# Spare matrix products of a one-core kernel moved: eleven groups more ahead of the first scores, thirteen fewer later

## The chip, the core and the metric

The kernel runs on one core of a Trainium2 chip. A core has five engines that run side by side: TensorE (matrix products, the page's PE, with its weight loads as PEld), VectorE (DVE), ScalarE (ACT), GpSimd (POOL) and SyncE (SP), which here only issues transfers. Each engine takes its instructions in the order in which they were written for it, and waits at an instruction until the data it needs are there. The metric is the device time of one execution in microseconds, as the median of several runs. Beside it there is a profile of one execution.

## The reference

Two blocks in a row. The first is a gated linear recurrence over 768 tokens for 4 sequences and 8 heads of width 48:

```
f = 1 / (1 + exp(-f_logit))
for t in range(S):
    state = f[t] * state + outer(k[t], v[t])
    y[t]  = q[t] @ state
```

The second takes the heads' outputs side by side as x (4 x 768 x 384), mixes with a two-dimensional Fourier transform, and ends in a two-layer network with a residual:

```
mixed = real(fft(fft(x, tokens), channels))
u  = x + mixed
un = (u - mean(u)) / sqrt(var(u) + 1e-6)
out = u + relu(un @ w_ch1) @ w_ch2
```

All values are f32; w_ch1 is 384 x 1536 and w_ch2 1536 x 384.

## The kernel before, in words

The recurrence is done in 16 units, each two heads of one sequence, and 6 chunks of 128 tokens. Of one unit, `attention` computes: the gate's logarithm (ScalarE, L330 and L331), its running sum W (a VectorE scan, L337), the exponentials (ScalarE, L342, L343, L345), q and k scaled with them (VectorE, L349 and L350), and the scores within a chunk (48 small products on TensorE, L361, into two PSUM buffers), which VectorE copies under a causal mask (L368). Then `outputs`: TensorE turns k (L506), ScalarE copies it out (kT, L508), TensorE forms the chunks' states (ds, L517), VectorE runs them through a scan (stt, L525), TensorE adds up y from the scores (L537) and from the states (L544), ScalarE copies y out (L553 to L557), TensorE turns it (yt, L564), ScalarE copies that into x (L566), and `fold` prepares sums and differences for the Fourier transform (L590 to L612, VectorE and GpSimd).

Once the four units of a sequence are through, `fnet` does the transform as products with tables (z, L650; mix, L669), adds it to x (L725, L728), and normalises (L691 to L709); `projected` does the network: the first layer L750 with its ReLU on ScalarE (L752), the second L759 or, in blocks, L773. The weights are loaded in a raw form by SyncE (L267) and converted (ScalarE L238, VectorE L240 and L241, GpSimd L242).

The buffers tie these together. g and k have three buffers for the units to come, q four, W and kT two each, and the scores, states and turned matrices share two PSUM buffers. A load of a later unit is issued by SyncE only once the earlier unit has done with the buffer, and all loads behind it in SyncE's order wait too.

The order of all work is written out by hand in the string ORDER. Each word runs one step and so adds its instructions to the engines' queues: a number is the next step of that unit, F, H and P are steps of `fnet`, of the normalisation and of `projected` for a sequence, L are loads, r, R fetch raw weights, C converts one block of them, T and S bring the tables, W combines weights. The word D calls `busy`, which issues four products whose results are never used:

```
for _ in range(4):
    nc.tensor.matmul(spare, lhsT=bound[:, :C], rhs=bound[:, :2 * C], start=not started, stop=True,
                     skip_group_check=True)
```

They are 128 x 128 by 128 x 256 in bf16. Their output is 256 columns of the PSUM area that also holds y; the operand, `bound`, is ready once GpSimd has filled it (L138). A group that stands behind a unit's y products waits, in the kernel as built, for ScalarE's last copy of that y (L557). Nothing reads what they write; their purpose is to keep TensorE busy while it would otherwise stand still.

Of the kernel before, what the change touches and what calls it, by code (L numbers as in the profile page):

```python
# [12 lines left out]
C = 128  # L13
# [11 lines left out]


ORDER = (
    "Gq2 r I D Gq0 L0f Gk1 L1f D Gk0 L0q i D Gq3 C Gq1 Z L0k 0 D 1 Gk2 0 L1q 1 L1k D 0 0 1 0 r 1 L2f 0 2 "
    "C L1v 1 L3fk D 1 3 L0v 0 1 L2q 2 0 0 r D 1 L2k 3 1 0 2 r 3 L3q 2 L2v D 0 C L3v D C L4fk R D 4 2 2 3 "
    "1 0 C 2 4 1 3 L5qv D L4qv L5fk 3 D D 3 2 0 2 3 2 3 C r 4 1 4 L6fk C r 2 5 4 D L6qv 4 D 2 1 5 6 3 4 "  # L30
    "D 4 C 5 3 D T 3 6 4 5 5 4 2 r L7fk 7 5 D L7qv 3 5 S L8fk C 4 7 6 6 5 F0 5 r r F0 F0 F0 7 4 C F0 "
    "L9fk 5 6 8 H0 H0 6 5 6 r D D H0 D C L8qv 6 7 L9qv P0 6 7 r C P0 7 7 C 9 P0 r r 5 8 C r C F0 r 7 F0 "
    "6 P0 5 9 C 6 7 P0 r C P0 8 8 C P0 r r 7 P0 P0 8 9 H0 C P0 P0 8 7 8 C P0 H0 7 D 9 6 H0 H0 C 9 r C P0 "
    "9 L10fk r 9 P0 r C 9 L11fk 10 C 6 P0 11 4 P0 P0 P0 P0 P0 P0 10 P0 P0 P0 L10qv P0 P0 7 F1 9 P0 F1 H0 "
    "9 W P0 D P0 P0 11 F1 P0 L11qv P0 P0 P0 9 P0 P0 P0 8 L12fk P0 11 11 8 P0 P0 10 11 F1 P0 11 11 10 "
    "L14fk F1 8 P0 14 F1 P0 10 P0 8 10 P0 P0 H1 H1 10 L12qv P0 P0 10 P0 F1 P0 11 11 10 P0 10 H1 P0 P0 P0 "
    "P0 12 12 12 P0 P0 12 P0 H1 P0 12 P0 H1 L13fk P1 P1 P1 P1 P1 14 13 P1 12 8 8 P1 P1 12 9 10 L13qv 13 "
    "P1 P1 L14qv 9 P1 12 11 P1 H1 11 10 P1 P1 13 P1 13 P1 12 P1 P1 14 P1 14 V 13 P1 c V 10 P1 P1 P1 P1 "
    "P1 V L15fk P1 13 P1 11 V P1 P1 P1 P1 c P1 11 F2 V c F2 F2 H1 13 H1 F2 c 14 P1 c V c P1 P1 12 P1 P1 "
    "14 P1 P1 13 V V V P1 15 F2 c P1 12 P1 P1 P1 P1 c P1 H2 14 15 V V P1 P1 P1 P1 P1 13 P1 14 F2 P1 c P1 "  # L40
    "P1 15 V 13 P1 H2 P1 P1 L15qv P1 14 13 P1 V 12 H2 F2 14 P2 P2 P2 P2 P2 P2 P2 15 P2 P2 P2 c c 12 H2 V "
    "H2 15 H2 15 P2 c P2 15 P2 P2 15 P2 14 13 15 P2 P2 14 P2 P2 15 13 P2 P2 P2 P2 P2 H2 V 15 P2 P2 14 15 "
    "H2 P2 P2 P2 P2 15 F3 F3 P2 F3 F3 P2 F3 c P2 P2 P2 P2 P2 V P2 c P2 V c c V P2 P2 P2 P2 P2 c P2 F3 F3 "
    "P2 V P2 H3 P2 P2 P2 H3 H3 P2 P2 P2 P2 P2 P2 P2 P2 P2 P2 P3 H3 c P3 P3 P3 P3 V P3 c P3 P3 P3 c V V c "
    "P3 P3 P3 H3 P3 P3 P3 P3 P3 P3 c P3 P3 V P3 H3 P3 P3 P3 P3 P3 P3 H3 H3 P3 P3 P3 P3 P3 P3 P3 P3 P3 P3 "
    "P3 P3 V P3 P3 P3 P3 P3 c P3 c P3 P3 P3 M P3 P3 P3 P3 P3 P3 P3 P3 P3 P3 P3 P3"
)

PAIRS = ((0, 3), (2, 5), (1, 4))
# [925 lines left out]
```

## Time and profile before

| | |
|---|---|
| median time | 557.96 us (3 runs, 557.95 to 559.05) |
| span of the profiled execution | 556.9 us |
| mean granted TensorE clock | 0.976 of full |
| TensorE busy | 529.4 us (95%), 4194 products |
| VectorE busy | 299.8 us (54%) |
| ScalarE busy | 192.6 us (35%) |
| GpSimd busy | 95.4 us (17%) |
| spare products (L153) | 92, from 3.9 to 155.6 us, 16.4 us busy in all |

The profile's page has the span in 40 slices of 13.9 us, with each engine's busy share of a slice in tenths, the clock that TensorE was granted, and the busy share of the 16 transfer engines. A timeline gives instructions with start and duration in us and, in brackets, the idle time of the engine ahead of them with the instruction or transfer that released it. A busy matrix engine isn't always at full speed: the same product takes longer at a lower clock, so durations and the clock are read together.

Where the 23 words D of the kernel before stand in the trace: five from 3.9 to 8.4 us; one each at 19.2, 22.8 and 25.4 us; two at 28.9; three at 38.1; two at 49.0; one each at 54.1, 58.6 and 62.8; two at 86.0 and one at 87.2; one each at 119.8 and 155.0 us.

### The profile page before, as it was taken

To read this page: it belongs to the slowest core of one execution; us is meant where nothing else is said; L and a number is where in the kernel's file an instruction comes from. 1 tells how busy PE (TensorE), PEld (TensorE's weight loads), DVE (VectorE), ACT (ScalarE), POOL (GpSimd) and SP (SyncE) were. 2 spreads that over 40 slices of the span, in tenths; PEclk is the share of its full clock that TensorE was granted. 3 is DMA by queue.
4 is the path that set the end of the run, shared out by engine and by line. 5 is a ranking of instruction groups with operands and counts; after the bars stand their busy time and mean duration, and the time that the engine had idled before them with its cause. 6 is when DMAs were issued, how large, how long until landed. Compare 5 with 4: busy or idle time off the path is not lost.

```text
span 556.9 us, 10217 instructions
## 1 busy us (share of the span) xinstructions
PE 529.4 (95%) x4194; PEld 464.4 (83%) x4194; DVE 299.8 (54%) x534; ACT 192.6 (35%) x497; POOL 95.4 (17%) x147
## 2 busy tenths in 40 slices
PE   3988699999999999999999999999999999999995
PEld 2877578886889889889889899899889798989985
DVE  8989899994845626445554443453443342413231
ACT  6757476573313433443240331321421302121110
POOL 6136642634101000140200000103001000010000
PEclk9788889999999999999999999999999999999999
DMA  8969636343402010310630301102002005000000
GB/s 223 257 172 245 195 106 172 126 145 106 118 1 58 15 44 2 115 44 23 219 114 15 114 1 51 36 1 87 1 28 86 0 2 171 0 29 0 29 2 34
DMA packets 18398, 44.38 MB, mean 80 GB/s; under 512 B 3109, under 2 KB 4710, under 8 KB 18342
## 3 DMA queue, kind: packets, MB, share of 16 engines
q1 hardware_dynamic: 17094, 39.89, 25.4%
q0 software_dynamic: 1104, 3.54, 1.8%
q8 instruction: 35, 0.57, 0.4%
q14 instruction: 21, 0.17, 0.1%
q10 hardware_dynamic: 144, 0.20, 0.1%
HBM read 38.90 MB, written 4.72 MB: 78 GB/s over the span
## 4 chain that ended last, share of the span: by engine, by line
PE 85%; DMA 7%; DVE 4%; ACT 1%; SPq 1%; issue 1%; POOL 0%; ACTq 0%; DVEq 0%; POOLq 0%
PE up L750 34%; PE fx L773 15%; PE fz L773 12%; PE z L650 4%; DMA g<-in_qkf_dram 3%; PE po L759 3%; PE mix L669 3%; PE sc L361 3%; PE y L537 3%; PE y L544 3%; DMA k<-in_qkf_dram 2%; PE ds L517 2%; PE pt L708 1%; PE yt L564 1%; DMA tab<-in_seq_tab_dram 1%; PE st L506 1%
## 5 line engine op out<-in xcount | busy, mean ns | idle before, releaser
L750 PE MATMUL up<-unT,w 128*128 128x256 f32 x864 | 197.1, 382 | 1.5 <-DVE x L728 0.9
L750 PEld LDWEIGHTS up<-unT,w 128*128 128x128 f32 x864 | 161.3, 190 | 25.7 <-issue 1.5
L752 ACT ACTIVATE h<-up 128x256 f32<-128x256 f32 x144 | 55.1, 383 | 200.5 <-PE up L750 194.3
L617 POOL DMA_INDIRECT out_dram<-x,place x16 | 16.9, 1056 | 270.7 <-DVE x L803 235.2
L773 PE MATMUL fx<-block,h 128*128 128x192 f32 x264 | 46.5, 326 | 0.0
L773 PE MATMUL fx<-w,h 128*128 128x192 f32 x264 | 44.9, 327 | 0.1
L773 PEld LDWEIGHTS fx<-w,h 128*128 128x128 f32 x264 | 43.1, 190 | 0.8 <-ACT h L752 0.4
L773 PEld LDWEIGHTS fx<-block,h 128*128 128x128 f32 x264 | 43.5, 190 | 0.0
L242 POOL TENSOR_TENSOR w<-w,raw 128x384 uint32<-128x384 uint32 x24 | 29.0, 1211 | 51.8 <-ACT raw L238 21.3
L780 DVE TENSOR_TENSOR s<-h,h 128x768 f32<-128x768 f32 x11 | 10.5, 954 | 50.8 <-ACT h L752 50.8
L361 PE MATMUL sc<-q,W 48*64 48x128 f32 x768 | 28.1, 297 | 6.7 <-DVE W L350 5.2
L368 DVE COPY_PREDICATED at<-causal,sc 128x768 f32<-128x768 uint32 x32 | 31.4, 1033 | 4.2 <-PE sc L361 4.1
L361 PEld LDWEIGHTS sc<-q,W 48*64 48x64 f32 x768 | 23.9, 147 | 10.8 <-DVE W L350 5.6
L337 DVE TENSOR_TENSOR_SCAN W<-g,bound 112x768 f32<-112x768 f32 x16 | 28.3, 1767 | 1.2 <-PE st L506 0.9
L725 DVE TENSOR_TENSOR x<-mix,x 128x384 f32<-128x384 f32 x12 | 6.7, 556 | 39.1 <-PE mix L669 39.1
L537 PE MATMUL y<-at,v 128*64 128x128 f32 (+1 forms) x384 | 24.9, 278 | 0.0
L537 PEld LDWEIGHTS y<-at,v 128*64 128x64 f32 (+1 forms) x384 | 21.3, 132 | 3.0 <-issue 3.0
L153 PE MATMUL y<-bound 128*128 128x256 bf16 x92 | 16.4, 334 | 7.6 <-POOL bound L138 3.9
L773 PE MATMUL fz<-w,s 128*128 128x192 f32 x132 | 23.5, 328 | 0.0
L773 PE MATMUL fz<-block,h 128*128 128x192 f32 x132 | 23.5, 328 | 0.0
L773 PE MATMUL fz<-w,h 128*128 128x192 f32 x132 | 23.4, 327 | 0.0
L544 PE MATMUL y<-q,stt 48*48 48x128 f32 x320 | 22.1, 283 | 0.0
(145 smaller groups left out, 742.9 us busy)
## 6 DMA issues: line engine op xcount, KB each, us to landing
raw<-in_w_ch_dram SPq DMA_DIRECT2D x24, 384.0 KB, 4.4
g<-in_qkf_dram SPq DMA_DIRECT2D x32, 144.0 KB, 4.1
q<-in_qkf_dram SPq DMA_DIRECT2D x32, 144.0 KB, 4.0
k<-in_qkf_dram SPq DMA_DIRECT2D x32, 144.0 KB, 4.3
v<-in_v_dram SPq DMA_DIRECT2D x16, 288.0 KB, 4.7
k<-in_w_ch_dram SPq DMA_DIRECT2D x12, 384.0 KB
g<-in_w_ch_dram SPq DMA_DIRECT2D x12, 384.0 KB, 5.1
out_dram<-x SPq DMA_DIRECT2D x4, 168.0 KB
```

What stands on the lines that cost most here:

```text
L242: nc.gpsimd.tensor_tensor(bits, bits, lo, ALU.add)
L337: nc.vector.tensor_tensor_scan(W, g, bound[:R], 0.0, ALU.add, ALU.min)
L361: nc.tensor.matmul(ps[64 * s:64 * s + 64, r, i * C:(i + 1) * C], lhsT=W[ROWS[r], o + 64 * s:o + 64 * s + 64], rhs=Q[ROWS[r], o:o + C], sta ...
L368: nc.vector.copy_predicated(AT[:, :, half], causal.bitcast(U32).unsqueeze(1).unsqueeze(1).to_broadcast([128, 2, NCH // 2, C]), ps[:, :, :N ...
L537: nc.tensor.matmul(y[FILL[r], c * C:(c + 1) * C], lhsT=vt[:, c, r * D:r * D + (64 if r == 0 else D)], rhs=AT[:, r, c], start=(c % 4 == 0), ...
L544: nc.tensor.matmul(y[ROWS[r], c * C:(c + 1) * C], lhsT=st[ROWS[r], :, c - 1], rhs=Q[ROWS[r], c * C:(c + 1) * C], start=False, stop=True, s ...
L617: nc.gpsimd.indirect_dma_start(out=out.rearrange("b s d -> (b s) d"), out_offset=bass.IndirectOffsetOnAxis(ap=place[:, b, i:i + 1], axis=0 ...
L650: nc.tensor.matmul(z[:, cols], lhsT=src[:, j, lo:hi], rhs=tab[:, t, T % 2, cols], start=(i == 0), stop=(i == len(parts) - 1), skip_group_c ...
L669: nc.tensor.matmul(mix[:, o], lhsT=zz[:rows_of[T], T, PLACES[c]], rhs=cd[:rows_of[T], T, :NQ - odd], start=(i == 0), stop=(i == 1))
L750: nc.tensor.matmul(pp[:, :256], lhsT=w1[:, kt, m * 128:(m + 1) * 128], rhs=unT[:, kt], start=(kt == 0), stop=(kt == 2))
L752: nc.scalar.activation(hs[-1][:, m % H].rearrange("p t n -> p (t n)"), pp[:, :256], AF.Relu)
L773: nc.tensor.matmul(out, lhsT=h[:, m], rhs=blocks[i][:, m], start=(start and m == 0), stop=(m == H - 1), skip_group_check=True)
```

## The change

Only the words D of ORDER move; all others keep their order. The fifth D, the one ahead of the first scores (`L1k D 0 0 1`), becomes twelve in a row, so that 64 spare products in place of 20 stand between the start and the first scores. Of the eighteen words after that, thirteen are taken out (those at 19.2, 22.8, 25.4, 28.9, 49.0, 58.6, 86.0, 87.2, 119.8 and 155.0 us), and five stay (three at 38.1, and those at 54.1 and 62.8 us). In all there are 21 words in place of 23, and 84 products in place of 92.

The intention is to keep TensorE working without a gap from the first moments up to the first scores, so that its clock is up when they come, and to spare the products where they stand in real work's way.

```diff
 ORDER = (
-    "Gq2 r I D Gq0 L0f Gk1 L1f D Gk0 L0q i D Gq3 C Gq1 Z L0k 0 D 1 Gk2 0 L1q 1 L1k D 0 0 1 0 r 1 L2f 0 2 "
-    "C L1v 1 L3fk D 1 3 L0v 0 1 L2q 2 0 0 r D 1 L2k 3 1 0 2 r 3 L3q 2 L2v D 0 C L3v D C L4fk R D 4 2 2 3 "
-    "1 0 C 2 4 1 3 L5qv D L4qv L5fk 3 D D 3 2 0 2 3 2 3 C r 4 1 4 L6fk C r 2 5 4 D L6qv 4 D 2 1 5 6 3 4 "
-    "D 4 C 5 3 D T 3 6 4 5 5 4 2 r L7fk 7 5 D L7qv 3 5 S L8fk C 4 7 6 6 5 F0 5 r r F0 F0 F0 7 4 C F0 "
-    "L9fk 5 6 8 H0 H0 6 5 6 r D D H0 D C L8qv 6 7 L9qv P0 6 7 r C P0 7 7 C 9 P0 r r 5 8 C r C F0 r 7 F0 "
-    "6 P0 5 9 C 6 7 P0 r C P0 8 8 C P0 r r 7 P0 P0 8 9 H0 C P0 P0 8 7 8 C P0 H0 7 D 9 6 H0 H0 C 9 r C P0 "
-    "9 L10fk r 9 P0 r C 9 L11fk 10 C 6 P0 11 4 P0 P0 P0 P0 P0 P0 10 P0 P0 P0 L10qv P0 P0 7 F1 9 P0 F1 H0 "
-    "9 W P0 D P0 P0 11 F1 P0 L11qv P0 P0 P0 9 P0 P0 P0 8 L12fk P0 11 11 8 P0 P0 10 11 F1 P0 11 11 10 "
...
+    "Gq2 r I D Gq0 L0f Gk1 L1f D Gk0 L0q i D Gq3 C Gq1 Z L0k 0 D 1 Gk2 0 L1q 1 L1k D D D D D D D D D D D "
+    "D 0 0 1 0 r 1 L2f 0 2 C L1v 1 L3fk 1 3 L0v 0 1 L2q 2 0 0 r 1 L2k 3 1 0 2 r 3 L3q 2 L2v 0 C L3v C "
+    "L4fk R 4 2 2 3 1 0 C 2 4 1 3 L5qv D L4qv L5fk 3 D D 3 2 0 2 3 2 3 C r 4 1 4 L6fk C r 2 5 4 L6qv 4 2 "
+    "1 5 6 3 4 D 4 C 5 3 T 3 6 4 5 5 4 2 r L7fk 7 5 D L7qv 3 5 S L8fk C 4 7 6 6 5 F0 5 r r F0 F0 F0 7 4 "
+    "C F0 L9fk 5 6 8 H0 H0 6 5 6 r H0 C L8qv 6 7 L9qv P0 6 7 r C P0 7 7 C 9 P0 r r 5 8 C r C F0 r 7 F0 6 "
+    "P0 5 9 C 6 7 P0 r C P0 8 8 C P0 r r 7 P0 P0 8 9 H0 C P0 P0 8 7 8 C P0 H0 7 9 6 H0 H0 C 9 r C P0 9 "
+    "L10fk r 9 P0 r C 9 L11fk 10 C 6 P0 11 4 P0 P0 P0 P0 P0 P0 10 P0 P0 P0 L10qv P0 P0 7 F1 9 P0 F1 H0 9 "
+    "W P0 P0 P0 11 F1 P0 L11qv P0 P0 P0 9 P0 P0 P0 8 L12fk P0 11 11 8 P0 P0 10 11 F1 P0 11 11 10 L14fk "
...
```

The rows left out hold no word D; they are the same words, moved along by the breaks of the lines.

## The prediction

> **What bounds the kernel now.** I read the page's 40 slices first. A slice is 13.9 us.
>
> ```profile
> PE   3988699999999999999999999999999999999995
> DVE  8989899994845626445554443453443342413231
> PEclk9788889999999999999999999999999999999999
> DMA  8969636343402010310630301102002005000000
> ...
> L153 PE MATMUL y<-bound 128*128 128x256 bf16 x92 | 16.4, 334 | 7.6 <-POOL bound L138 3.9
> ```
>
> From the sixth slice on TensorE is full. VectorE is nearly full through the first nine, to about 125 us. The first five slices (to 70 us) are bound by nothing steadily: TensorE has holes, its clock falls, and the transfers fill their engines. So a microsecond of TensorE work removed after 125 us is worth a microsecond; between 75 and 125 us only what VectorE can follow; before 70 us it depends on which wait ends last. The 92 spare products (23 words D of 4) lie in all three parts. TensorE's timeline for the opening:
>
> ```profile
> 3.94 4.43 PE L153 MATMUL y<-bound 128*128 128x256 bf16 x20 [3.94 <-POOL bound L138]
> 13.53 5.71 PE L361 MATMUL sc<-q,W 48*64 48x128 f32 x96 [5.16 <-DVE W L350]
> 19.18 1.04 PE L153 MATMUL y<-bound 128*128 128x256 bf16 x4
> 20.00 2.04 PE L506 MATMUL st<-ident,W 112*128 112x112 f32 x10
> ...
> 28.89 1.86 PE L153 MATMUL y<-bound 128*128 128x256 bf16 x8 [1.63 <-ACT yT L557]
> 30.68 2.21 PE L361 MATMUL sc<-q,W 48*64 48x128 f32 x48
> ```
>
> The columns are start, duration, instruction, and idle time before it with its releaser. Twenty spare products, a hole of 5.2 us, then the scores of units 0 and 1. At 28.89 eight spare products wait for ScalarE's copy of the outputs (L557) and hold the scores of unit 2 behind them. Next, the granted clock by stretch (columns: busy time of PE, PEld, DVE, ACT, POOL, then PEclk, DMA share and GB/s):
>
> ```profile
> 11.80:13.50 1.70, 0.00 (x0) 0.00 (x0) 1.68 (x2) 1.68 (x3) 0.00 (x0) 0.50 1.11 277
> 13.50:19.30 5.80, 5.73 (x97) 5.00 (x98) 5.65 (x7) 5.19 (x9) 0.83 (x1) 0.50 1.04 245
> ...
> 28.70:32.10 3.40, 3.21 (x36) 2.40 (x39) 1.09 (x3) 2.34 (x7) 2.21 (x2) 0.50 0.70 164
> ...
> 66.20:73.10 6.90, 5.17 (x42) 3.70 (x39) 6.52 (x16) 5.74 (x13) 4.62 (x12) 0.51 0.54 159
> ```
>
> Half clock from 11.8 to 21.9, 28.7 to 32.1, 49.2 to 52.6 and 66.2 to 73.1 us: about 24 us. Then, in the timeline of all engines, who stands where around 31 us:
>
> ```profile
> 27.15 0.95 DVE L350 TENSOR_TENSOR W<-W,k 112x768 f32<-112x768 f32 x1
> ...
> 30.94 0.84 ACT L330 ACTIVATE g<-g 112x768 f32<-112x768 f32 x1 [1.03 <-DMA g<-in_qkf_dram]
> ...
> 32.31 1.96 DVE L368 COPY_PREDICATED at<-causal,sc 128x768 f32<-128x768 uint32 x2 [2.49 <-PE sc L361]
> ```
>
> The factors that unit 2's scores need are there at 28.10 (L350); VectorE then idles 2.49 us for scores that start only at 30.68. Last, the chain that ended last, which goes through a transfer just ahead of the dense part:
>
> ```profile
> 56.30 10.72 DMA g<-in_qkf_dram
> 67.10 0.94 ACT g L330 x2
> ```
>
> [...] the stretches above last 10.1, 3.4, 3.4 and 6.9 us, multiples of 3.4. [...] The trace: (4.43 - 0.27)/19 = 219 ns each in the first twenty, (0.61 - 0.27)/3 = 113 ns at 22.75 us. So the first twenty ran cold although the clock column shows 1.00 there; I believe the durations. [...] here ScalarE's copy of kT at 68.82 indeed stands behind the L330 that waits for the transfer above.
>
> **The change part by part.** The words other than D keep their order exactly, so each engine's other instructions do too; D goes from 23 to 21 words, 92 to 84 products. Five words to the first scores become 16 in one run; of 18 later, five stay.
>
> *Eleven groups more before the first scores.* 44 products. The first twenty end at 8.37 as now. [...] Then 44 x 113 ns = 5.0 us, ending at 13.4, beside L350, which ends at 13.48 and lets the scores go: nothing on the path. [...] 32 would be cold and 32 warm: 3.94 + 32 x 0.219 + 32 x 0.113 = 14.6 us, 1.1 us late. Even then scores at warm pace (48 in 1.54 us at 47.51) give the first half by 15.4, when VectorE, busy without a break, reaches L368 (15.32). Cost 0 to 0.1 us; I take 0.
>
> *The removed group at 19.18.* Warm, unit 1's scores end as soon as L368 frees their buffers (about 18.2, now 19.24), and the transposes L506 of unit 0 start when L368 frees the next, about 19.3 instead of 20.00. VectorE waits 0.9 us for them before the scan L337 at 21.24. That goes: 0.9 us.
>
> *Those at 22.75 and 25.38* (0.45 us each) lie inside VectorE's chain: 0.
>
> *The two at 28.89.* With them gone the scores wait only for L350: 28.10 - 0.9 = 27.2 instead of 30.68, 3.5 us earlier. Not all of it goes on: the g of unit 4 lands at 30.94 out of transfers that have filled their engines since 4 us, and ScalarE's queue holds it (L330, L331 to 32.75) ahead of the copies L566 (35.11 now), L508 and L553 to L557. They can move by 35.11 - 32.75 = 2.4 us at most, while the chain through scores and L368 moves 3.4. The y products of unit 1 (end 36.83), which release SyncE's load of q at 36.86, move between these too, and with it the transfers that now pause from 34 to 38 us. I take 2.9, the middle.
>
> *Those at 48.98 and 58.63.* VectorE is busy 4.75 of 5 us and 4.97 of 5 in 50 to 60: 0, apart from the clock. The kept ones (38.06, 54.14, 62.81) cost as before.
>
> *What arrives at 70 us.* The g load whose landing at 67.02 releases ScalarE, and through kT TensorE's L517 at 69.48, follows in SyncE's queue after the load at 36.86; the stretch between is full of transfers but for 55 to 65 us, so it should carry the same 2.9.
>
> *Three groups at 86.00 and 87.20.* They hold TensorE 0.51 us of waiting plus 12 products, 1.3 us. The scores at 90.00 could come 1.3 us earlier (their L350 ends at 88.43). But VectorE idled only 0.61 us for them at 90.95, and at 120.77 TensorE meets VectorE's L705, which ends only at 120.58. So 0.6.
>
> *One at 119.76* is 0.45 us of TensorE; L705 leaves 0.2 of it. *One at 154.99*: TensorE full, VectorE 27 of 40 us busy: all 0.45.
>
> Sum: 2.9 + 0.6 + 0.2 + 0.45 = 4.15 (the 0.9 is inside the 2.9). 557.96 - 4.15 = 553.8 us.
>
> *The clock* is not in the sum. [...] Cold, the 8.6 us of other products between 52.6 and 66.2 could double, against 5 us of holes: some 3.6 us; the stage from 66 on already is cold now. In the other direction, a warm 66 to 73 us saves L517's 1.43 - 0.85 and the first z's 2.62 - 1.46, 1.7 us. Bounds: -1.7 to +6.
>
> **The rivals.**
>
> *A: all of it counts.* The shift is the full 3.4, the dense stage's 1.8 and 0.9 are kept, and 66 to 73 is warm: 3.4 + 1.8 + 0.9 + 1.7 = 7.8, so 550.2. For: no TensorE wait above 0.2 us stands between 71 and 120 us but the filler's own. Against: VectorE's load there.
>
> *B: the transfers take it.* The early gain dies at the landing at 67.02: the g issued at 56.30 took 10.7 us against a median 4.1, beside the gathered table of 8.3 us on GpSimd's queue. If that is set by bytes, 0.5 is left: 0.5 + 0.6 + 0.2 + 0.45 = 1.75, so 556.2. For: DMA share near 1 from 40 to 55. Against: it paused at 34 to 38, waiting for TensorE.
>
> *C: the clock takes more than it gives* (slower). The gain of 4.15 minus the 6 above: 559.8. [...] Against: two of the removed fillers at 28.89 and those at 48.98 ran cold themselves, and blocked[...].
>
> **How the numbers follow.** Forecast 0.48, A 0.15, B 0.22, C 0.15. The time is the forecast's, 553.8. The range leaves out the tail of A and most of C: 550.6 to 558.0. Faster by over 0.2% (below 556.8): forecast, A and three quarters of B, 0.79; within: the rest of B and the mild end of C, 0.08; slower 0.13.
>
> **What would show it.** Right: 64 products without a hole to about 13.4 us, the last 40 or so at 113 ns; clock 1.00 from 12 to at least 18 us; VectorE's 2.49 us wait for scores gone and unit 2's scores near 27 us; SyncE's q load near 34; z near 68; the landing of g near 64. Wrong: spare products still at 219 ns when the scores are due; clock at half in more than 24 us before 75; the landing of g still near 67, or ScalarE's kT behind it; TensorE waits on L368, L350 or L705 in 75 to 125 us that eat the removed groups. A hole that is filled but followed by half clock anyway would leave the first step without use, though the removal at 28.89 would still count.

## The result, and the profile after

The changed kernel takes 554.15 us (median of 4 runs, 553.52 to 554.99) beside 558.11 us before. The ratio is 0.9927, 95% interval 0.9909 to 0.9944: 4.0 us faster. The profiled executions span 552.4 us after 556.9; the one before was timed at 558.64 us, half a microsecond above its median, the one after at 554.13. The forecast was 553.8 us.

The slices of the page after, to be held against those before:

```profile
PE   6888699999999999999999999999999999999995
DVE  8999899984936427425644344444452442413231
PEclk9797799999999999999999999999999999999999
DMA  8989645363202100412530401002002004000001
```

The first slice of TensorE is at 6 in place of 3: that is the filled hole. The sixth to ninth slices are full as before. The clock's low spots are not gone, they have moved.

TensorE's timeline of the opening, after:

```profile
3.94 9.51 PE L153 MATMUL y<-bound 128*128 128x256 bf16 x64 [3.94 <-POOL bound L138]
13.78 1.54 PE L361 MATMUL sc<-q,W 48*64 48x128 f32 x48 [0.32 <-DVE W L350]
16.65 1.82 PE L361 MATMUL sc<-q,W 48*64 48x128 f32 x48 [1.33 <-DVE at L368]
19.37 2.13 PE L506 MATMUL st<-ident,W 112*128 112x112 f32 x10 [0.90 <-DVE at L368]
...
23.83 2.47 PE L537 MATMUL y<-at,v 128*64 128x128 f32 x23
26.23 1.34 PE L544 MATMUL y<-q,stt 48*48 48x128 f32 x20
28.01 1.54 PE L361 MATMUL sc<-q,W 48*64 48x128 f32 x48 [0.45 <-PE y L544]
```

All 64 spare products end at 13.45 us, and the scores of units 0 and 1 take 1.54 and 1.82 us for 48 each in place of 5.71 for 96. But between and after them TensorE waits 1.33 and 0.90 us for VectorE's masks, and the clock falls from 1.00 to 0.50 at about 19 us. The granted clock by stretch, after (the columns as before, clock third from the end):

```profile
18.00:20.00 2.00, 1.10 (x24) 0.86 (x14) 2.00 (x3) 0.97 (x3) 1.02 (x1) 0.76 1.03 231
20.00:22.00 2.00, 2.00 (x22) 1.66 (x21) 1.57 (x2) 1.09 (x2) 0.00 (x0) 0.50 1.07 275
22.00:24.00 2.00, 2.00 (x36) 2.00 (x35) 1.67 (x4) 1.42 (x3) 0.19 (x1) 0.50 1.03 258
24.00:26.00 2.00, 2.00 (x24) 2.00 (x21) 1.97 (x3) 1.26 (x3) 0.19 (x1) 0.53 1.03 264
...
65.00:70.00 5.00, 3.57 (x29) 2.17 (x25) 4.73 (x12) 4.88 (x13) 3.57 (x9) 0.50 0.68 191
```

Half clock from about 19 to 26 us raises the price of unit 0's y from 1.47 us for 23 products (full clock, before) to 2.47. Unit 2's scores are released by the y products ahead of them, at 28.01 us; before, they started at 30.68. VectorE's timeline at that place:

```profile
29.08 0.56 DVE L241 SCALAR_TENSOR_TENSOR w<-raw,w 128x384 uint32<-128x384 uint32 x1
29.55 1.98 DVE L368 COPY_PREDICATED at<-causal,sc 128x768 f32<-128x768 uint32 x2
```

No bracket stands behind L368: the wait of 2.49 us is gone, and the masks start 2.76 us earlier (29.55 against 32.31). From there the chain that ended last carries it on:

```profile
33.59 0.33 SPq L170
...
54.31 10.09 DMA g<-in_qkf_dram
...
64.48 0.94 ACT g L330 x2
...
66.86 1.44 PE ds L517 x18
68.29 6.38 PE z L650 x28
```

SyncE's load of q is issued at 33.59 in place of 36.86, the g transfer lands at 64.40 in place of 67.02, and the first z starts 2.6 us earlier (68.22 against 70.84 in TensorE's timeline). Last, TensorE's timeline where the next groups stood, before:

```profile
86.00 1.03 PE L153 MATMUL y<-bound 128*128 128x256 bf16 x8 [0.51 <-ACT yT L557]
86.88 0.49 PE L708 MATMUL pt<-ident,un 128*128 128x128 f32 x3
87.20 0.60 PE L153 MATMUL y<-bound 128*128 128x256 bf16 x4
...
90.00 1.54 PE L361 MATMUL sc<-q,W 48*64 48x128 f32 x48
```

and after:

```profile
83.17 0.55 PE L708 MATMUL pt<-ident,un 128*128 128x128 f32 x3 [0.39 <-DVE un L705]
83.81 0.85 PE L517 MATMUL ds<-v,kT 128*64 128x48 f32 x20
84.59 1.56 PE L750 MATMUL up<-unT,w 128*128 128x256 f32 x6
86.08 1.54 PE L361 MATMUL sc<-q,W 48*64 48x128 f32 x48
```

The scores that stood at 90.00 start at 86.08, 3.9 us earlier, so 1.3 more were won since the first z, 1.2 of them at the three groups and 0.1 in the z products (the row of yt in the table, where the turned y follows the z products). A table of such places, both profiles:

| start of | before | after | gained |
|---|---|---|---|
| scores of units 0 and 1 (L361) | 13.53 | 13.78 | -0.25 |
| scores of unit 2 (L361) | 30.68 | 28.01 | 2.7 |
| first z (L650) | 70.84 | 68.22 | 2.6 |
| yt after the z products (L564) | 77.24 | 74.51 | 2.7 |
| scores after the three groups (L361) | 90.00 | 86.08 | 3.9 |
| po (L759) | 122.99 | 118.70 | 4.3 |
| next z (L650) | 147.82 | 143.52 | 4.3 |
| first fx (L773) | 161.93 | 157.19 | 4.7 |
| end | 556.9 | 552.4 | 4.5 |

From the first fx on, the remaining 395 us take the same time in both, within 0.25 us. Everything happens ahead of it.

### The profile page after: what moved, and what is told of

Same layout as the page of the kernel before. It is cut to its first block, busy times and chain, and to the rows that moved or that the text cites. A ratio compares the mean times of both kernels' runs of the same rounds, so it can differ in the third digit from the quotient of the medians.

```text
span 552.4 us, 10204 instructions
## 1 busy us (share of the span) xinstructions
PE 528.4 (96%) x4186; PEld 463.3 (84%) x4186; DVE 298.6 (54%) x534; ACT 192.6 (35%) x497; POOL 95.5 (17%) x147
## 4 chain that ended last, share of the span: by engine, by line
PE 87%; DMA 4%; DVE 3%; ACT 2%; SPq 1%; POOL 1%; issue 1%; ACTq 0%; POOLq 0%
PE up L750 34%; PE fx L773 16%; PE fz L773 12%; PE z L650 4%; PE y L537 3%; PE y L544 3%; PE po L759 3%; PE mix L669 3%; PE sc L361 3%; PE ds L517 2%; DMA g<-in_qkf_dram 2%; PE yt L564 2%; PE pt L708 1%; DMA raw<-in_w_ch_dram 1%; PE st L506 1%; DMA tab<-in_seq_tab_dram 1%
## 5 line engine op out<-in xcount | busy, mean ns | idle before, releaser
L773 PE MATMUL fx<-block,h 128*128 128x192 f32 x264 | 46.5, 326 | 0.0
L773 PE MATMUL fx<-w,h 128*128 128x192 f32 x264 | 44.9, 327 | 0.1
L773 PEld LDWEIGHTS fx<-w,h 128*128 128x128 f32 x264 | 43.1, 190 | 0.8 <-ACT h L752 0.4
L773 PEld LDWEIGHTS fx<-block,h 128*128 128x128 f32 x264 | 43.5, 190 | 0.0
L242 POOL TENSOR_TENSOR w<-w,raw 128x384 uint32<-128x384 uint32 x24 | 30.3, 1267 | 47.6 <-ACT raw L238 19.1
L368 DVE COPY_PREDICATED at<-causal,sc 128x768 f32<-128x768 uint32 x32 | 31.2, 1030 | 0.8 <-PE sc L361 0.8
L337 DVE TENSOR_TENSOR_SCAN W<-g,bound 112x768 f32<-112x768 f32 x16 | 28.0, 1751 | 1.6 <-issue 0.9
L361 PE MATMUL sc<-q,W 48*64 48x128 f32 x768 | 24.9, 273 | 3.7 <-issue 1.4
L725 DVE TENSOR_TENSOR x<-mix,x 128x384 f32<-128x384 f32 x12 | 6.7, 556 | 39.0 <-PE mix L669 39.0
L361 PEld LDWEIGHTS sc<-q,W 48*64 48x64 f32 x768 | 20.9, 133 | 7.5 <-issue 3.6
L537 PE MATMUL y<-at,v 128*64 128x128 f32 (+1 forms) x384 | 26.9, 292 | 0.0
L537 PEld LDWEIGHTS y<-at,v 128*64 128x64 f32 (+1 forms) x384 | 23.2, 140 | 3.0 <-issue 3.0
L773 PE MATMUL fz<-w,s 128*128 128x192 f32 x132 | 23.5, 328 | 0.0
L773 PE MATMUL fz<-block,h 128*128 128x192 f32 x132 | 23.5, 328 | 0.0
L773 PE MATMUL fz<-w,h 128*128 128x192 f32 x132 | 23.4, 327 | 0.0
L773 PEld LDWEIGHTS fz<-w,s 128*128 128x128 f32 x132 | 21.6, 190 | 0.3 <-issue 0.3
```

Of the source, the lines that this page charges most:

```text
L242: nc.gpsimd.tensor_tensor(bits, bits, lo, ALU.add)
L337: nc.vector.tensor_tensor_scan(W, g, bound[:R], 0.0, ALU.add, ALU.min)
L361: nc.tensor.matmul(ps[64 * s:64 * s + 64, r, i * C:(i + 1) * C], lhsT=W[ROWS[r], o + 64 * s:o + 64 * s + 64], rhs=Q[ROWS[r], o:o + C], sta ...
L368: nc.vector.copy_predicated(AT[:, :, half], causal.bitcast(U32).unsqueeze(1).unsqueeze(1).to_broadcast([128, 2, NCH // 2, C]), ps[:, :, :N ...
L537: nc.tensor.matmul(y[FILL[r], c * C:(c + 1) * C], lhsT=vt[:, c, r * D:r * D + (64 if r == 0 else D)], rhs=AT[:, r, c], start=(c % 4 == 0), ...
L773: nc.tensor.matmul(out, lhsT=h[:, m], rhs=blocks[i][:, m], start=(start and m == 0), stop=(m == H - 1), skip_group_check=True)
```

## The experiments

The first question was which part of the change pays: the removals that let ready work go (my theory, "blocked work"), or the filled hole with its warm clock (the rival). Each edit is given as its part of ORDER; `D x 12` means twelve words in a row. Times are medians; the ratio is to the kernel before, measured beside it. That took 558.00 us beside the first four variants below (removals, fill, two groups, late five), 558.64 beside those at 49.0 and 58.6 us, the bridges, the ten groups and the changed kernel again, and 558.38 beside the rest.

**Removals without the fill.**

```diff
  ORDER of the changed kernel, but
- L1k D x 12 0 0 1
+ L1k D 0 0 1
```

> The thirteen later groups are out, but only the five early ones stand ahead of the first scores, so the hole of 5 us at 8.4 to 13.5 us is open again. Theory (blocked work): the gain comes from taking spare products out of the way of ready work, so this keeps nearly all of it: 553.6 to 555.0 us; the clock falls to half near 12 us, the scores of units 0 and 1 run cold as before, yet unit 2's scores start at 27.5 to 28.5 us. Rival (warm clock): the filled hole carries the gain; without it 556 to 557.5 us, and unit 2's scores after 29 us.

Measured: 553.63 us, ratio 0.9933 (0.9915 to 0.9952). By the medians 3.7 of the 4.0 us are there without the fill; the changed kernel measured again, further down, gained 5.0, so that a microsecond for the fill is not excluded. The TensorE timeline:

```profile
13.69 5.71 PE L361 MATMUL sc<-q,W 48*64 48x128 f32 x96 [5.66 <-DMA raw<-in_w_ch_dram]
19.49 2.28 PE L506 MATMUL st<-ident,W 112*128 112x112 f32 x10
...
28.28 1.54 PE L361 MATMUL sc<-q,W 48*64 48x128 f32 x48 [1.19 <-issue]
```

The first scores run at half clock (0.50 from 12 to 20 us) and take 5.71 us, as before, and yet unit 2's start at 28.28, only 0.3 us after those of the changed kernel, since VectorE, busy 5.65 of the 5.8 us of those scores in the kernel before, paces units 0 and 1.

**The fill without the removals.**

```diff
  ORDER of the kernel before, but
- L1k D 0 0 1
+ L1k D x 12 0 0 1
```

> Only the eleven groups more ahead of the first scores; all eighteen later ones stay. Theory (blocked work): 557.3 to 558.3 us, since VectorE sets when the first masks are copied and the two groups at 28.9 us still stand in front of unit 2's scores (start 29.5 to 30.7 us). Rival (warm clock): 555 to 556 us.

Measured: 555.79 us, ratio 0.9966 (0.9953 to 0.9979). My theory's expectation failed and the rival's came true. The timeline of all engines shows how (lines of this kernel are one higher, since ORDER takes one row more: L154 is the spare product, L362 the scores, L369 the mask):

```profile
27.84 1.03 PE L154 MATMUL y<-bound 128*128 128x256 bf16 x8 [1.62 <-ACT yT L558]
...
28.80 1.54 PE L362 MATMUL sc<-q,W 48*64 48x128 f32 x48
29.76 1.97 DVE L369 COPY_PREDICATED at<-causal,sc 128x768 f32<-128x768 uint32 x2 [0.98 <-PE sc L362]
```

The two groups still block, but here, with the groups at 19, 23 and 25 us in place, the granted clock is 1.00 from 12 to 55 us, where the changed kernel, without them, has 0.50 from 19 to 26: y comes sooner, its copy is done a microsecond sooner, and the eight products take 1.03 us instead of 1.86. Unit 2's scores start at 28.80 and the first z at 67.96. So the fill alone reaches nearly the same place by another way, and at this place the two don't add up: 28.80 with the fill, 28.28 with the removals, 28.01 with both, 30.68 with neither. The medians point the same way (1.9 us for the fill alone, 3.7 for the removals alone, 4.0 and 5.0 for both), but their intervals would let the two add.

**The two groups at 28.9 us alone, twice.**

```diff
  ORDER of the kernel before, but
- C L3v D C L4fk R D 4 2 2 3
+ C L3v C L4fk R 4 2 2 3
```

> The kernel before without the two groups at 28.9 us alone. Theory: unit 2's scores start near 28.2 us instead of 30.7, the load of q at 36.9 us comes 2 to 2.6 us earlier, and this carries to the end: 555.4 to 556.0 us. Rival (the transfers or VectorE take it on the way to 70 us): 557 to 558 us.

Measured: 557.74 us, ratio 0.9996 (0.9981 to 1.0010): in the rival's range, outside my theory's. The profiled execution of the same kernel told another story: unit 2's scores at 27.90, the first z at 67.55 (3.3 us earlier), the span 554.3 us; but it was the second fastest of 14 (556.03 us). So it was run again.

> The kernel before without the two groups at 28.9 us, once more, for a second profile. Its first profile had unit 2's scores 2.8 us earlier and ended 2.6 us earlier, while the median of its runs moved by 0.3 us. If the gain is lost between 45 and 75 us to half clock in most executions, this profile shows it: time 556.5 to 558.5 us, and half clock in more of that stretch.

Measured: 555.92 us, ratio 0.9968 (0.9948 to 0.9988); scores of unit 2 at 27.96, z at 67.64, span 554.2. The time lies below the range expected. Both profiles agree on the way to the first z: two groups out, 3 us earlier there. The two ratios overlap only between 0.9981 and 0.9988; taken together the gain at the end is about 1 us, less than my 2.0 to 2.6. TensorE's timeline of the first profile shows two places where an earlier start is lost again:

```profile
67.55 2.13 PE L650 MATMUL z<-tab,se 128*95 128x385 f32 x6 [2.21 <-POOL half L207]
69.47 2.57 PE L650 MATMUL z<-tab,xs 128*96 128x385 f32 x6
...
74.52 0.74 PE L564 MATMUL yt<-ident,yT 112*128 112x112 f32 x6
```

The first z waits 2.21 us for GpSimd (L207), which is putting the Fourier tables in order (so it does in the removals without the fill, 2.22 us, and in the variant without the five groups from 19 to 29 us, 1.62). The g is there early in this execution: ScalarE starts on it at 61.95 us, 5.1 earlier than before, and z can use only 3.3 of that. In the changed kernel the same L207 ends 0.8 us ahead of z, so this second path to the first z is close behind the g there too; my working didn't have it. Then the first two sets of z products take 2.13 and 2.57 us, largely at half clock (a mean of 0.83 in both 65 to 70 and 70 to 75 us, so 3.4 us of it), against 2.62 and 1.46 in the kernel before: from z to yt it is 6.97 us in both profiles, against 6.40 before. From yt on nothing is lost (45.75 us to po in both, as before).

Why the runs of one kernel differ by up to 3.5 us was not settled. Half clock for more of 45 to 75 us, as I expected, isn't what the second profile shows (it has about 10 us of it, as the kernel before has), and of the six runs over 558 us in the first measurement four had a higher mean clock (0.986 to 0.989) than the profiled one (0.980). In the profiles of both kernels the difference between executions lies ahead of yt: from there to the end they agree within 0.1 us.

**The late five alone.**

```diff
  ORDER of the kernel before, but without the words D of
- r D D H0 D C      (86.0, 86.0, 87.2 us)
- H0 7 D 9 6        (119.8 us)
- 9 W P0 D P0       (155.0 us)
```

> The kernel before without the five groups at 86.0, 86.0, 87.2, 119.8 and 155.0 us alone. By the trace of the changed kernel TensorE comes out 1.2 us ahead at the first three, 0.4 at the fourth and 0.45 at the last: 555.9 to 556.1 us. Rival (VectorE holds TensorE back between 75 and 125 us, as forecast at first): 0.6 + 0.2 + 0.45 = 1.25, so 556.7 us. If the groups keep a clock up that later work needs: over 558 us.

Measured: 556.45 us, ratio 0.9978 (0.9959 to 0.9997), so 1.2 us with an interval of 0.2 to 2.3, which holds both theories. Its profile has z at 70.82, just where it stood, po 2.0 us earlier (120.97) and the first fx 2.5 us earlier (159.47). Of that, 0.5 comes from z products at full clock in this execution (yt at 76.78 in place of 77.24), and 2.0 from the groups, as the first theory has it. TensorE's timeline:

```profile
85.44 0.55 PE L708 MATMUL pt<-ident,un 128*128 128x128 f32 x3 [0.39 <-DVE un L705]
...
88.35 1.54 PE L361 MATMUL sc<-q,W 48*64 48x128 f32 x48
```

VectorE does hold TensorE now (0.39 us at L705), but for no more than that. The price of the late five repeats in the profiles of all kernels here, whatever happened ahead of 75 us:

| | with the late five | without |
|---|---|---|
| yt after the z products to po, us | 45.74 to 45.88 (7 profiles) | 44.17 to 44.19 (7 profiles) |
| po to the first fx, us | 38.93 to 38.94 (7) | 38.49 to 38.50 (6) |

So the first four of them cost 1.6 us and the one at 155.0 us 0.44: 2.0 in all.

**The groups at 49.0 and 58.6 us alone.**

```diff
  ORDER of the kernel before, but
- 2 5 4 D L6qv 4 D 2 1
+ 2 5 4 L6qv 4 2 1
- 5 3 D T 3
+ 5 3 T 3
```

> The kernel before without the two groups at 49.0 us and the one at 58.6 us alone. Theory (VectorE is full there and hides them, as forecast): 557.4 to 558.4 us. Rival (they hold the turned y of units 2 and 3 and through it the first Fourier stage): 555.5 to 556.8 us. If they were needed for the clock: over 558.6 us.

Measured: 558.51 us, ratio 0.9992 (0.9976 to 1.0008). Nothing that shows, as forecast.

**The five groups from 19 to 29 us alone.**

```diff
  ORDER of the kernel before, but
- 1 L3fk D 1 3 ... 0 0 r D 1 L2k ... 2 L2v D 0 C L3v D C L4fk R D 4
+ 1 L3fk 1 3 ... 0 0 r 1 L2k ... 2 L2v 0 C L3v C L4fk R 4
```

> The kernel before without the five groups at 19.2, 22.8, 25.4 and 28.9 us (two) alone. The removals ahead of 70 us are worth about 2.8 us together (removals only against the late five out), and the three at 49 and 58 us nothing. Theory (the five stand in one chain up to unit 2's scores and count together): 555.0 to 556.2 us. Rival (the early gain [...] averages out, as it did for the two at 28.9 us alone): 557.3 to 558.5 us.

Measured: 556.49 us, ratio 0.9971 (0.9953 to 0.9990), 1.6 us. A little above the theory's range and below the rival's, though the interval (555.8 to 557.8 us beside 558.38) reaches into both. With 0.4 for the three at 49 and 58 (not clear of nothing) and 1.2 for the late five, the parts make 3.2 us against 3.7 for all removals together: they add up within their intervals.

**The fill with fillers to bridge the holes after it.** Now the two sources of gain were to be joined: full clock, and nothing in the way.

```diff
  ORDER of the kernel before, but
- L1k D 0 0 1
+ L1k D x 12 0 0 1
  and without the two D at 28.9 us and the late five
```

> The filled hole, and of the later groups the seven that stand before no ready work at 28.9 us or in the full stages: those at 19.2, 22.8, 25.4, 49.0 (two), 58.6 and the five that the change kept stay; the two at 28.9 us and the late five are out. Theory (the fill counts only while fillers after it keep the clock up): full clock from 9 to 45 us, unit 2's scores near 27.5 us, and a time below both the changed kernel and the removals alone: 552.0 to 553.4 us. Rival (clock is of no use once the blocking groups are gone): 553.5 to 554.5 us.

Measured: 554.73 us, ratio 0.9925 (0.9903 to 0.9946). The clock came out as wished (by stretch):

```profile
12.00:20.00 8.00, 6.50 (x124) 4.94 (x121) 7.93 (x11) 6.96 (x13) 1.02 (x1) 1.00 1.05 248
20.00:28.00 8.00, 6.76 (x126) 5.64 (x130) 7.67 (x11) 6.35 (x14) 0.38 (x2) 1.00 1.04 258
28.00:52.00 24.00, 20.35 (x361) 17.07 (x354) 22.66 (x33) 16.41 (x35) 13.27 (x15) 1.00 0.99 241
52.00:60.00 8.00, 4.66 (x76) 3.98 (x74) 6.31 (x8) 2.79 (x8) 5.28 (x10) 0.86 0.76 206
```

Full clock to past 52 us, unit 2's scores at 27.19: and no gain over the changed kernel (553.92 us beside it). That theory fell; the time lies a little above the rival's range too. VectorE is busy 7.93 of 8, 7.67 of 8 and 22.66 of 24 us there and the transfers nearly without a break (DMA share 1.05, 1.04 and 0.99); unit 4's scores stand at 44.68, against 44.74 in the changed kernel, 44.64 with only the two groups out and 44.95 with only the fill. Two variants without the fill stand later, at 46.05 (removals only) and 45.27 (the next one below). In the others TensorE's speed in the first 50 us is not what the later start waits for, once nothing blocks.

**No spare products after the first scores.**

```diff
  ORDER of the removals without the fill, and also
- L5qv D L4qv L5fk 3 D D 3 ... 3 4 D 4 C ... 7 5 D L7qv
+ L5qv L4qv L5fk 3 3 ... 3 4 4 C ... 7 5 L7qv
```

> Five groups ahead of the first scores as before and none after, so 20 spare products in all. Theory (the five kept groups at 38, 54 and 62 us stand where TensorE waits anyway): the same as removals only, 553.2 to 554.4 us. Rival (they keep the clock up on the way to the full stage): 555 to 557 us.

Measured: 554.36 us, ratio 0.9934 (0.9914 to 0.9954). The five groups that the change kept neither cost nor bring anything that shows.

**Ten groups in the full stage.**

```diff
  ORDER of the changed kernel, but
- 9 W P0 P0 P0 11
+ 9 W P0 D x 10 P0 P0 11
```

> The changed kernel with ten groups put in at the place of the one that stood at 155.0 us, in the middle of full TensorE work. It measures the price of a group there: ten times 0.44 us, so 4.4 us over the changed kernel, 558.2 to 558.9 us. If a spare product were hidden even there: below 556 us.

Measured: 559.83 us, ratio 1.0024 (1.0009 to 1.0039), 5.7 us above the changed kernel's 554.15, and 5.9 above the 553.92 of the same kernel beside it, where 4.4 were expected. TensorE's timeline:

```profile
149.99 4.53 PE L153 MATMUL y<-bound 128*128 128x256 bf16 x40
154.36 2.75 PE L750 MATMUL up<-unT,w 128*128 128x256 f32 x12
```

40 products take 154.36 - 149.99 = 4.37 us, 0.44 a group: the price is right. Of the rest, the profile shows one longer wait between 300 and 400 us, 1.6 us for ScalarE's L709 against 0.3; what links it to the ten groups stays open.

**The same kernels again.** First the changed kernel:

> The changed kernel once more, beside the others on one chip, for more of its runs: 553.6 to 554.6 us by both theories; its clock stretches may lie elsewhere than in its first profile.

Measured: 553.92 us, ratio 0.9911 (0.9889 to 0.9933). Its profile, of the slowest of its six runs (556.32 us, span 554.5), by stretch:

```profile
28.00:32.00 4.00, 4.00 (x70) 3.50 (x60) 3.96 (x7) 2.57 (x7) 2.20 (x2) 0.67 0.88 187
56.00:64.00 8.00, 7.57 (x86) 6.39 (x86) 5.57 (x12) 0.64 (x1) 3.64 (x9) 0.57 0.64 167
64.00:76.00 12.00, 9.44 (x62) 6.70 (x61) 11.35 (x20) 7.37 (x22) 7.20 (x12) 0.72 0.61 168
```

The same program has half clock at places where its first profile had none (within 28 to 33 and most of 56 to 63 us), z at 69.09 instead of 68.22, yt at 76.68 instead of 74.51, and ends 2.1 us later. All of the difference lies ahead of yt. Then the kernel before:

> The kernel before against itself, for a second profile of it and for the size of a difference that is none: 557.3 to 559 us, ratio within 0.2% of 1, half clock in 20 to 30 us of the first 75.

Measured: 558.07 us, ratio 1.0005 (0.9986 to 1.0025), z at 70.40, yt at 76.36. That is the size of no difference. The second pair of profiles also warns against reading the early gain out of a single pair: at z it shows 1.3 us where the first pair showed 2.6, and at yt none (76.36 and 76.68). Its gain of 1.6 us in the span is that of the late groups.

## Why the prediction was right, point by point

The time (553.8 against 554.15 us) and most of its way came as written, but two terms of the sum were mis-sized in opposite directions, so that its closeness is in part luck.

*The first scores.* Forecast: 64 products end at 13.4, no cost. Seen: 13.45, then 0.32 us of waiting for L350. That the faster pace would set in right after the first twenty was my estimate, and close: the first 24 start 0.21 us apart, up to 8.81 us, the others 0.109 us apart. But the zero was a zero for this change only: without the removals the fill is worth 1.9 us, which nothing in my working said.

*The group at 19.18.* Forecast 0.9 us at the scan L337; seen 20.66 in place of 21.24, 0.6. VectorE still idles 0.43 us ahead of the scan, with the turned products at half clock (2.13 us for ten; 0.70 for five in the bridged variant).

*The two at 28.9.* Forecast: unit 2's scores at 27.2, then 2.4 to 3.4 us carried on, 2.9 taken. Seen: 28.01, since the clock fell at 19 us (27.19 in the variant where it did not), SyncE's load 3.3 us earlier (33.59; "near 34" was said), the landing at 64.40 (64), z at 68.22 (68): 2.6. The way to z is shown in both profiles of the two groups taken out alone, z 3 us earlier each time; its worth at the end, taken alone, is nearer 1 us. The working took an earlier z for an earlier end one to one, and that is its weakest link: GpSimd's tables stand close behind (0.8 us in the changed kernel), and the first z products can fall into half clock (2.13 and 2.57 us for the first two sets in the profile above). By the medians the whole change gained 4.0 us (5.0 measured again), and the late groups 2.0 of them, which leaves 2.0 to 3.0 for this early term. Why it differs between executions stays open.

*The clock after the fill.* The profile was to show 1.00 from 12 to at least 18 us: it did, to 19. That half clock would come where removed fillers leave TensorE partly idle was my estimate. It came from 19 to 26 us, after 1.77 us of work in the 3.40 us up to 19.0 (in the kernel before, the 3.40 us ahead of half clock at 28.7, 49.2 and 66.2 us held 1.96, 1.94 and 1.70 us of work), and cost little: unit 2's scores stand 0.8 us later than in the bridged variant with its clock of 1.00 to past 52 us, unit 4's 0.06.

*49 and 58 us.* Forecast 0; alone 0.9992 (0.9976 to 1.0008).

*The dense stage.* This term was mis-sized: 0.6 us for the three groups and 0.2 for the fourth, with VectorE named as what takes the rest. Measured from yt on, the three groups gave 1.2 us of the 1.8 that TensorE spent on them (0.51 of waiting and 1.3 of products), and the fourth 0.4 of its 0.45. VectorE's timeline before:

```profile
88.63 0.76 DVE L525 TENSOR_TENSOR_SCAN stt<-ds,te 112x288 f32<-112x288 f32 x1 [0.20 <-PE ds L517]
...
90.95 1.96 DVE L368 COPY_PREDICATED at<-causal,sc 128x768 f32<-128x768 uint32 x2 [0.61 <-PE sc L361]
```

and after:

```profile
87.31 1.96 DVE L368 COPY_PREDICATED at<-causal,sc 128x768 f32<-128x768 uint32 x2
```

The mask that stood at 90.95 came at 87.31 with no wait, 1.0 us more than z had gained. The working counted only the 0.61 us of idle time just before it; 0.20 more stood at L525 and 0.17 at L725 (0.56 before, 0.39 after). VectorE is busy 95% of 75 to 125 us, and the rest was enough. VectorE took something, as forecast (0.39 us at L705), but less. By the medians, the late five alone are worth 1.2 us with an interval that holds both 1.25 and 2.0; the profiles, which agree within 0.15 us, decide for 2.0. The group at 155.0 gave 0.44 us, as forecast.

*The rivals.* B (the transfers keep the early gain) did not happen: the landing moved 2.6 us with the issue's 3.3. C (colder, slower) did not: the mean granted clock went from 0.976 to 0.981. A failed at its clock term, half clock (0.50) still lay over 65 to 70 us; the 2.0 seen in the dense stage lies midway between its 2.7 and my 1.25.

*The sum.* By the first pair of profiles the terms come to 2.7 up to yt + 1.2 + 0.4 + 0.4 = 4.7, and the span shrank by 4.5; the medians say 4.0, the forecast was 4.15. Two errors of opposite sign stand in it: 2.9 early, where the medians leave 2.0 (3.0 in the repeat) and the first profiles show 2.6 at z, and 1.25 late for 2.0.

## What to carry to other kernels

A filler instruction is a real one to everything behind it in its queue (1.63 us of waiting and 1.86 of products ahead of unit 2's scores here): look first at what it waits for, and at what ready work stands behind that wait. Full clock is worth what the engine's speed is worth at that place (to past 52 us it brought the bridged variant nothing, 554.73 us beside 553.92); where another engine paces, filling a hole and clearing the way can be two roads to the same microseconds, and their gains need not add (unit 2's scores at 28.80, 28.28 and, with both, 28.01 us). When executions differ by where half clock falls, let many runs decide how much, and profiles only how; a stage whose length repeats within 0.15 us in every profile, though, is priced better by the profiles.

## What the runs showed of the hardware that was not expected

The clock fell within a stretch in which TensorE was far from idle: between 13.8 and 19.4 us of the changed kernel it was busy with 96 products for about 3.3 of 5.6 us (1.77 of the last 3.40 us before the fall), and half clock came at about 19. In the bridged variant, with one group of fillers right behind the same scores (18.15 us) and two more up to 25 us, it stayed at 1.00. The other way round, a busy stretch did not always end the half clock: in the kernel before TensorE was busy for 3.36 of the 3.40 us from 15.2 to 18.6 us, with the small products of the first scores, and half clock lasted to 21.9 us. The same program got its half clock at partly different places in two executions (19 to 26, 46 to 53 and 63 to 70 us in one; 19 to 22.5, within 28 to 33, 46 to 50, 56 to 63 and 67 to 73 in the other), and its time went from 552.4 to 554.5 us of span. And the clock column showed 1.00 for the first spare products, which by their spacing of 0.213 us ran at about half of the rate seen later (0.109 us).
